# Inverse roots of the first attention's norms: from GpSimd's power to ScalarE's logarithm and exponential with a Newton step on VectorE

## Chip, core and metric

One core of a Trainium2 chip runs the whole program. The metric is the device time of one execution in microseconds, as a median over runs.

## What is computed

Attention with normalised queries and keys, followed by a feed-forward block with a squared ReLU:

```python
def rmsnorm(x, g):
    rms = np.sqrt(np.mean(x * x, axis=-1, keepdims=True) + 1e-06)
    return x / rms * g
q_n, k_n = (rmsnorm(q, g_q), rmsnorm(k, g_k))        # (8, 12, 448, 64)
scores = 1.0 / np.sqrt(64) * np.matmul(q_n, k_n.transpose(0, 1, 3, 2))
attn = softmax(scores)                                # over the keys
x = np.matmul(attn, v)                                # -> (8*448, 12*64)
out = np.maximum(x @ w_in, 0.0) ** 2 @ w_out          # 768 -> 2048 -> 768
```

The change concerns 1 / rms, the inverse root of the mean square over 64 values of a head's row, for queries and keys.

## The kernel before

Heads are handled in pairs: 8 batches x 6 pairs make 48 pairs. Two batches form a span; there are four spans. The first span's attention (pairs 0 to 11, `attention_alone`) runs by itself at the start of the program; the attention of each later span is interleaved with the second matrix product of the span before it, where TensorE is full of other work. The order of all instructions is written out by hand (`manual_schedule`): each engine takes its own instructions in program order, and semaphores hold an instruction until what it reads or overwrites is ready.

Both matrix products of the feed-forward block use a two-level scheme with seven products instead of eight, and the weight blocks for it (sums and differences of quarters) are made on the chip during the first attention and the first product. The generator `prepare(t)` hands this work out in four ticks a step: ScalarE takes absolute values and scales (L578, L594), VectorE works on exponents and signs (L591, L596, L601), GpSimd joins the words (L566) and adds blocks (L572), and SP writes finished blocks to DRAM (L586). The loop around `attention_alone` calls `weights(...)` at every `yield`, so these ticks are strewn through the iterations.

An iteration i of `attention_alone`, on TensorE: scores of key chunks 0 and 1 (L767), transposes of the normed keys of pair i+1 (L742), the values of pair i-1 for its last two chunks (L825), transposes of the normed queries of pair i+1 (L742), scores of chunks 2 and 3, the softmax totals of pair i-1 (L850, six matmuls for odd i and four for even i, each recorded twice by the profile), the values of pair i for its first two chunks. Scores live in two banks, so the scores of the next iteration wait for the exponentials of chunks 2 and 3. ScalarE takes in the same iteration, in this order: exponentials of chunks 0 and 1 (L771, four instructions), the copy of the transposed keys out of PSUM (L744), the squares for pair i+2 (L698), the copy of the transposed queries (L746), exponentials of chunks 2 and 3; the weights' ticks fall between. The transposed keys and queries of a pair share one PSUM bank, so the transposes of the queries wait for L744.

The norm of pair i+2 is made in iteration i by `norm`: ScalarE squares queries and keys (L698), VectorE sums over 64 (L699) and scales and adds epsilon (L700), GpSimd takes the power -0.5 of the 16 columns (L702) and multiplies the queries by it (L704); the keys' root is applied later as the scale of the exponentials. Pairs 0 to 2 use `normalise_in_turn` instead, with queries and keys one after the other; pairs from 12 on use `norm_by_squares`, which also has a power on GpSimd (L724) in another layout. Neither of the two is changed.

On VectorE an iteration also has the sums of probabilities (`add_up`, L784), and `finish` for pair i-1 (L863 to L874: transpose the totals, reciprocal, transpose back, multiply). `combine_x` (L884, L887 to L889) prepares sums of inputs for the first product from pair 6 on.

At the start of the program a 1x1 exponential (L1229) makes ScalarE load its table before data is there.

Of the kernel before, what the change touches and what calls it, by code (L numbers as in the profile page):

```python
# [2 lines left out]

# [6 lines left out]
F32 = mybir.dt.float32  # L10
U32 = mybir.dt.uint32
AF = mybir.ActivationFunctionType
ALU = mybir.AluOpType
# [290 lines left out]
def places_of(qk, i, work):  # L304


    first, second = i % 2 * 4 + work, i % 2 * 4 + 2 + (i // 2 + work) % 2
    return qk[:, first:second + 1:second - first]
# [78 lines left out]
def attention_then_ffn_bounded(  # L387
# [35 lines left out]
    nc = tc.nc  # L423

    B, H, S, D = q.shape
    NT, DM = out.shape
    DFF = w_in.shape[1]
    P = 128
    NJ = 4
    SP = S // NJ  # L430
# [11 lines left out]
    NAT = 2 * NPAIR  # L442
# [9 lines left out]
    small = ctx.enter_context(tc.tile_pool(name="small", bufs=2))  # L452
# [11 lines left out]
    qk, qkT, ident, mhalf, gains, rstd0, _ = held  # L464
# [189 lines left out]
    vs, probs, pavs, tots, normed, rstds = {}, {}, {}, {}, {}, {0: rstd0}  # L654
    places, halves, rests = [], [], {}
    sums = {"out": [dram.tile([2 * S // 32, 32], F32, name=f"factors{n}") for n in range(2)]}
# [20 lines left out]
    def load_v(i):  # L677
        b, h0 = i // NPAIR, 2 * (i % NPAIR)
        vs[i] = loads.tile([P, 2, NJ, D], F32, tag="vt", name="vt")
        if i < NAT:  # L680
            nc.sync.dma_start(vs[i][:SP].rearrange("p h j d -> p h (j d)"),
                              v[b, h0:h0 + 2].rearrange("h (p j) d -> p h (j d)", j=NJ))
        else:
            for h in range(2):
                nc.sync.dma_start(vs[i][:, h, 0:NF], v[b, h0 + h, 0:NF * P].rearrange("(j p) d -> p j d", j=NF))
            for rows in sides:
                nc.sync.dma_start(vs[i][rows, :, NF], v[b, h0:h0 + 2, NF * P:].rearrange("h p d -> p h d"))

    def norm(i):
        if i >= NAT:  # L690
            squares(i)
            return norm_by_squares(i)
        raw, sq = (places_of(qk, i, n)[:SP] for n in range(2))
        rstd = rstds[i] = small.tile([SP, 2, 2 * NJ], F32, tag="rstd", name="rstd", bufs=4)
        normed[i] = sq[:, 0], raw[:, 1]
        if i <= 2:
            return normalise_in_turn(nc, raw, sq, rstd, mhalf)
        nc.scalar.activation(sq, raw, AF.Square)  # L698
        nc.vector.tensor_reduce(rstd, sq.rearrange("p s (n d) -> p s n d", d=D), AX, ALU.add)  # L699
        nc.vector.tensor_scalar(rstd, rstd, 1.0 / D, 1e-6, ALU.mult, ALU.add)  # L700
        flat = rstd.rearrange("p s n -> p (s n)")
        nc.gpsimd.tensor_tensor(flat, flat, mhalf[:SP, 0:4 * NJ], ALU.pow)  # L702

        nc.gpsimd.tensor_tensor(sq[:, 0].rearrange("p (j h d) -> p h j d", j=NJ, h=2),  # L704
                                raw[:, 0].rearrange("p (h j d) -> p h j d", j=NJ, h=2),
                                rstd[:, 0].rearrange("p (h j) -> p h j ()", h=2).to_broadcast([SP, 2, NJ, D]),
                                ALU.mult)
# [131 lines left out]
    def added(i):  # L839

        return 3 if i % 2 and i + 1 < NAT else 2
# [49 lines left out]
    def attention_alone():  # L891


        for i in range(NAT):
            more = i + 1 < NAT
            if 0 < i < NAT - 3:
                load(i + 3)
            scores(i, 0)
            scores(i, 1)
            if i == 0:  # L900

                transpose(1, 1, 1)
                scores(0, 2)
                scores(0, 3)
                transpose(1, 0, 0)
                add_up(0, 1)
                norm(2)
                load_v(1)
                values(0, (0, 1))
                load(3)  # L910
                yield
                continue
            if more:
                transpose(i + 1, 1, 0)
            values(i - 1, (2, 3))
            add_up(i, 1)
            if i + 2 < NAT:
                norm(i + 2)
            elif not more:
                norm(NAT)  # L920
                load(NAT + 2)
            yield
            if more:
                transpose(i + 1, 0, 0)
            load_v(i + 1)
            yield
            scores(i, 2)
            scores(i, 3)
            total_of(i - 1)
            values(i, (0, 1))  # L930
            finish(i - 1)
            yield
            if added(i) == 3:
                add_up(i, 2)
            combine_x(i - 1)
            if NAT <= i + 3 < NAT + 2:
                load(i + 3)
            yield
        values(i, (2, 3))
        total_of(i)  # L940
        finish(i)
        combine_x(i)
# [185 lines left out]
    with tc.tile_pool(name="words", bufs=2) as spare["pool"]:  # L1128
        load(2)
        for _ in range(2):  # L1130
            load_w(loaded[0])
            loaded[0] += 1
        norm(1)
        with tc.tile_pool(name="first", bufs=2, reuse_waits="tile") as work:

            free = [gT[:, f] for f in range(NFC) if f % HF < HF - 2]
            places[:] = [g.rearrange("p (h q) -> p h q", h=2) for g in free[:2 * NJ]]
            sums[0], sums[1] = (g.rearrange("p (h q) -> p h q", h=2) for g in free[2 * NJ:2 * NJ + 2])
            sums["turned"], sums["factors"] = (g[:, 0:S] for g in free[2 * NJ + 2:2 * NJ + 4])
            sums["ones"] = work.tile([SP, D], F32, tag="ones", name="ones", bufs=1)  # L1140
            nc.vector.memset(sums["ones"], 1.0)
            for u, _ in enumerate(attention_alone()):

                weights(min(EARLY, 4 + (EARLY - 4) * u // (4 * NAT - 7)))
                if u == 4 * NAT - 9:
                    load_blocks(5)
        with tc.tile_pool(name="first_product", bufs=2, reuse_waits="tile") as work:
            for u, _ in enumerate(first_product(work, 0)):
                if u == 6:

                    left = ps_s.tile([P, 2, 512], F32, tag="s", name="bits")
                    banks["bits"] = left.rearrange("p a b -> p (a b)")[:, 0:NW].bitcast(U32)
                weights(min(ALL, EARLY + (ALL - EARLY) * (u - 1) // (N1 - 6)))
                if u == N1 - 5:
                    norm(NAT + 1)
                if u == N1 - 4:
                    transposes(NAT)
                    squares(NAT + 2)
# [25 lines left out]
def kernel(  # L1184
# [17 lines left out]
    nc = tc.nc  # L1202
    S, D = q.shape[-2:]
    bound = ctx.enter_context(tc.tile_pool(name="bound", bufs=1))
    gg = bound.tile([1, 2, D], F32, name="gg")
    top = bound.tile([1, 1], F32, name="top")
# [18 lines left out]
    )  # L1225
    with tc.manual_schedule():

        nc.vector.memset(top, 0.0)
        nc.scalar.activation(top, top, AF.Exp)  # L1229
        first_pair(tc, q, k, g_q, g_k, held)  # L1230

    bits = nc.values_load(top.bitcast(mybir.dt.int32))
# [37 lines left out]
```

## Time and profile before

| what | us |
|---|---|
| median of 3 runs (lowest, highest) | 1368.19 (1366.46, 1371.15) |
| the profiled execution: its time | 1369.76 |
| the profiled execution: its span, first to last instruction | 1367.8 |
| TensorE busy in 20.00 to 66.28 us | 44.75 of 46.28 |
| TensorE busy in 66.28 to 109.50 us | 38.93 of 43.22 |
| TensorE busy in 109.50 to 137.00 us | 25.00 of 27.50 |
| TensorE busy in 137 to 262 us (first product) | 124.47 of 125.00 |
| TensorE busy from 262 us to the end | 1092.27 of 1105.80 |

The first attention lasts from about 9 us to 133 us. A row of the profile gives an engine's busy time; an idle engine is listed with what ended its wait, as read from the semaphores. Instructions that ran on TensorE have modelled ends, so a gap of a tenth of a microsecond is at the limit of what can be read.

The granted TensorE clock is full in every slice of the span. ScalarE's busy time in the first 133 us is made of these groups, among others (busy us, mean ns of one, then the idle time before them):

```profile
L771 ACT ACTIVATE gT<-sc,rstd 112x448 f32<-112x448 f32 x96 | 53.1, 645 | 14.7 <-PE sc L767 11.5 <-issue 1.7 <-POOL rstd L702 1.5
L698 ACT ACTIVATE qk<-qk 112x1024 f32<-112x1024 f32 x9 | 9.8, 1084 | 2.8 <-DMA qk<-in_k_dram 2.8
L746 ACT ACTIVATE qkT<-pt,gains 128x448 f32<-128x448 f32 x11 | 7.1, 646 | 3.3 <-PE pt L742 3.3
L744 ACT COPY qkT<-pt 128x448 f32<-128x448 f32 x11 | 6.0, 548 | 0.0
```

### The profile page before, as it was taken

How to read it: one execution, taken by the hardware profiler on the slowest of the kernel's cores; microseconds unless marked ns; L12 is line 12 of the kernel's file. 1: busy time of each engine (PE TensorE's matmuls, PEld its weight loads, DVE VectorE, ACT ScalarE, POOL GpSimd, SP SyncE). 2: the span in 40 equal slices, each digit the busy share in tenths (PEclk: the TensorE clock that was granted, in tenths of full speed). 3: DMA queues.
4: the chain of work that ended last, by engine and by line, in shares of the span. 5: the costliest groups of instructions: out<-in, count | busy, mean ns of one | idle time of the engine just before them, and what ended most of it. 6: DMA issues, size and time to landing. Idle time of an engine off the chain costs nothing.

```text
span 1367.8 us, 16894 instructions
## 1 busy us (share of the span) xinstructions
PE 1341.9 (98%) x5602; PEld 638.1 (47%) x5602; DVE 811.9 (59%) x1434; ACT 426.8 (31%) x657; POOL 633.2 (46%) x505
## 2 busy tenths in 40 slices
PE   8989999999999999999999999999999999999997
PEld 3333454444444455444444455444444445554553
DVE  6989776499986334467778523467788533332111
ACT  7875565433332011233332011233433101110000
POOL 6998887455563122555564122545666312220000
PEclk9999999999999999999999999999999999999999
DMA  9787998655675333446676433345765433333443
GB/s 245 194 234 198 329 390 291 184 117 118 133 141 126 97 86 87 102 113 136 130 140 121 111 93 87 100 110 106 157 124 114 99 91 89 90 90 101 106 114 66
DMA packets 434021, 190.12 MB, mean 139 GB/s; under 512 B 282885, under 2 KB 430725, under 8 KB 433925
## 3 DMA queue, kind: packets, MB, share of 16 engines
q1 hardware_dynamic: 425476, 180.10, 52.2%
q0 software_dynamic: 4736, 8.40, 2.4%
q8 instruction: 47, 0.77, 0.2%
q10 hardware_dynamic: 3712, 0.46, 0.2%
q14 instruction: 50, 0.40, 0.1%
HBM read 155.72 MB, written 33.16 MB: 138 GB/s over the span
## 4 chain that ended last, share of the span: by engine, by line
PE 86%; POOL 6%; DVE 4%; DMA 2%; issue 2%; ACT 1%; DVEq 0%; POOLq 0%; ACTq 0%
PE ps L1086 35%; PE pa L1039 10%; PE pd L1039 10%; PE pc L1039 10%; PE sc L759 7%; PE pav L836 6%; PE pb L1039 5%; POOL rstd L702 2%; POOL gC L566 1%; POOL gC L572 1%; DMA xT<-factors 1%; POOL qk L704 1%; DMA sw<-w1s 1%; ACT gT L771 0%; PE tot L850 0%
## 5 line engine op out<-in xcount | busy, mean ns | idle before, releaser
L1086 PE MATMUL ps<-gT,sw 128*128 128x448 f32 x768 | 301.1, 545 | 4.7 <-DVE p L1105 4.0
L1016 POOL TENSOR_TENSOR gT<-gT 128x448 f32<-128x448 f32 x96 | 93.9, 980 | 290.6 <-ACT gT L1012 290.6
L1086 PE MATMUL ps<-gC,sw 128*128 128x448 f32 x576 | 225.2, 542 | 0.0
L1086 PEld LDWEIGHTS ps<-gT,sw 128*128 128x128 f32 x768 | 144.4, 191 | 156.3 <-issue 145.6
L724 POOL TENSOR_TENSOR half<-half,mhalf 128x28 f32<-128x28 f32 x36 | 174.5, 4847 | 75.3 <-DVE half L723 72.1
L1086 PEld LDWEIGHTS ps<-gC,sw 128*128 128x128 f32 x576 | 108.0, 190 | 113.0 <-issue 110.1
L1039 PE MATMUL pa<-xT,sw 128*128 128x448 f32 x384 | 154.9, 539 | 0.0
L1012 ACT ACTIVATE gT<-gT 128x448 f32<-128x448 f32 x96 | 55.4, 577 | 311.6 <-DVE gT L1054 311.5
L761 ACT ACTIVATE pr<-sc 128x896 f32<-128x896 f32 x87 | 77.4, 915 | 121.5 <-PE sc L759 121.5
L759 PE MATMUL sc<-qkT 64*64 64x448 f32 (+1 forms) x1152 | 109.7, 496 | 0.0
L1039 PEld LDWEIGHTS pa<-xT,sw 128*128 128x128 f32 x384 | 72.9, 190 | 71.7 <-issue 70.3
L804 POOL DMA_DIRECT2D xT<-factors x72 | 38.0, 532 | 90.1 <-DMA factors<-square 61.0
L1054 DVE TENSOR_TENSOR gT<-z,pd 128x448 f32<-128x448 f32 x32 | 19.8, 620 | 99.7 <-PE pd L1039 99.6
L1039 PE MATMUL pb<-xC,sw 128*128 128x448 f32 x192 | 77.6, 540 | 1.4 <-issue 1.4
L1039 PE MATMUL pc<-xT,sw 128*128 128x448 f32 x192 | 77.5, 540 | 0.5 <-DMA sw<-w1s 0.5
L1039 PE MATMUL pd<-xT,sw 128*128 128x448 f32 x192 | 77.8, 541 | 0.0
L1039 PE MATMUL pc<-xC,sw 128*128 128x448 f32 x192 | 77.5, 540 | 0.0
L1039 PE MATMUL pd<-xC,sw 128*128 128x448 f32 x192 | 77.4, 539 | 0.0
L726 POOL TENSOR_TENSOR qk<-qk,half 128x448 f32<-128x448 f32 x72 | 75.0, 1061 | 2.8
L572 POOL TENSOR_TENSOR gC<-gC 128x384 f32<-128x384 f32 x64 | 73.2, 1162 | 2.5
L836 PE MATMUL pav<-pr,vt 64*64 64x448 f32 x348 | 72.7, 537 | 1.5 <-DVE half L872 1.5
L836 PE MATMUL rest<-pr,vt 64*64 64x448 f32 x348 | 72.7, 537 | 0.0
(135 smaller groups left out, 1879.7 us busy)
## 6 DMA issues: line engine op xcount, KB each, us to landing
sw<-w1s SPq DMA_DIRECT2D x224, 192.0 KB, 2.4
sw<-w2s SPq DMA_DIRECT2D x168, 256.0 KB, 3.2
w1s<-gC SPq DMA_DIRECT2D x8, 1344.0 KB, 7.5
w2s<-gC SPq DMA_DIRECT2D x8, 1344.0 KB, 8.1
out_dram<-osb SPq DMA_DIRECT2D x184, 56.0 KB, 1.9
qk<-in_q_dram SPq DMA_DIRECT2D x144, 56.0 KB, 3.6
qk<-in_k_dram SPq DMA_DIRECT2D x144, 56.0 KB, 2.9
xT<-factors POOLq DMA_DIRECT2D x72, 112.0 KB, 3.4
```

Source lines behind the costliest of these rows:

```text
L572: nc.gpsimd.tensor_tensor(*[blocks_of(n)[:, i] for i in (dst, x, y)], op)
L702: nc.gpsimd.tensor_tensor(flat, flat, mhalf[:SP, 0:4 * NJ], ALU.pow)
L724: nc.gpsimd.tensor_tensor(half, half, mhalf, ALU.pow)
L726: nc.gpsimd.tensor_tensor(qkn[:, s], raw[:, s], half[:, s * NG:(s + 1) * NG].rearrange("p g -> p g ()").to_broadcast([P, NG, 32]), ALU.mult)
L759: nc.tensor.matmul(sc[part, h, 0:n], qkT[rows, 0, 1, keys], qkT[rows, 0, 0, of], start=True, stop=True)
L761: nc.scalar.activation(pr, sc[:, :, 0:n], AF.Exp)
L804: nc.gpsimd.dma_start(xT[h * D:(h + 1) * D, b % 2, hp], sums["out"][i % 2].rearrange("(h g) t -> h () (g t)", h=2)[h].to_broadcast([D, S]))
L836: nc.tensor.matmul(into, vs[i][rows, h, c, :], probs[i, c][rows, h, :], start=(c == 0), stop=(c == NF), skip_group_check=True)
L1012: nc.scalar.activation(g, src, AF.Relu)
L1016: nc.gpsimd.tensor_tensor(g, g, g, ALU.mult)
L1039: nc.tensor.matmul(ps, stream[n + i][:, c], rhs[:, c], start=first and c == 0, stop=c == HC - 1, skip_group_check=not first)
L1086: nc.tensor.matmul(ps, stream[n][:, c % 4], rhs_of[i][:, c], start=c == 0, stop=c == HF - 1)
```

## The change

For pairs 3 to 11 `norm` ends after the scaling (L700). The roots and the product with the queries move to a new function `roots`, which is called one `yield` later in the same iteration, behind the transposes of the queries of pair i+1 and the load of v. There ScalarE computes ln(x / 2^63) and from it exp(-0.5 ln(x / 2^63) - 31.5 ln 2), which is the inverse root; VectorE improves it by one Newton step in three operations, y (1.5 - 0.5 x y^2); and GpSimd's product with the queries follows as before. Two small tiles are used for it, of the tags that `norm_by_squares` uses too. The bias of the exponential gets a tile of its own, set once by VectorE. At the start of the program the 1x1 memset and exponential are replaced by an explicit preload of the table set that has logarithm and exponential. Between `norm` and `roots` of the same pair lies one call of `weights`, so in most iterations a tick's instructions come between them on each engine.

```diff
@@ norm, pairs from 3 on
         nc.scalar.activation(sq, raw, AF.Square)
         nc.vector.tensor_reduce(rstd, sq.rearrange("p s (n d) -> p s n d", d=D), AX, ALU.add)
         nc.vector.tensor_scalar(rstd, rstd, 1.0 / D, 1e-6, ALU.mult, ALU.add)
+
+    def roots(i):
+        raw, sq = (places_of(qk, i, n)[:SP] for n in range(2))
+        rstd = rstds[i]
         flat = rstd.rearrange("p s n -> p (s n)")
-        nc.gpsimd.tensor_tensor(flat, flat, mhalf[:SP, 0:4 * NJ], ALU.pow)
-
+        y, t = (small.tile([P, 2 * S // 32], F32, tag=tag, name=tag)[:SP, 0:4 * NJ] for tag in ("half", "other"))
+        nc.scalar.activation(y, flat, AF.Ln, scale=2.0 ** -63)
+        nc.scalar.activation(y, y, AF.Exp, scale=-0.5, bias=sums["rebias"])
+        nc.vector.scalar_tensor_tensor(t, y, -0.5, flat, ALU.mult, ALU.mult)
+        nc.vector.tensor_tensor(t, t, y, ALU.mult)
+        nc.vector.scalar_tensor_tensor(flat, t, 1.5, y, ALU.add, ALU.mult)
         nc.gpsimd.tensor_tensor(sq[:, 0].rearrange("p (j h d) -> p h j d", j=NJ, h=2),
...
@@ attention_alone
             if more:
                 transpose(i + 1, 0, 0)
             load_v(i + 1)
+            if i + 2 < NAT:
+                roots(i + 2)
             yield
@@ before the loop over attention_alone
+            sums["rebias"] = work.tile([SP, 1], F32, tag="rebias", name="rebias", bufs=1)
+            nc.vector.memset(sums["rebias"], -31.5 * math.log(2.0))
@@ start of the program
-        nc.vector.memset(top, 0.0)
-        nc.scalar.activation(top, top, AF.Exp)
+        nc.scalar.preload_act_table_set("natural_log_exp_and_others")
```

More of the change, by code (lines that the diff above doesn't have):

```diff
@@ L1 @@
+import math
 import struct
```

## The prediction

> **What bounds the kernel now.** I read the page first (shares by engine, then the chain), then the waits of TensorE in the stage that the change touches, then that stage cut into its iterations, and last the timeline of the iterations that are too long. TensorE is busy for 98% of the span, so the most that any edit can give is its idle time, 1367.8 - 1341.9 = 25.9 us, and only the part of it that lies in the first attention. Columns below: busy us, share, instructions.
>
> ```profile
> PE 1341.9 (98%) x5602; PEld 638.1 (47%) x5602; DVE 811.9 (59%) x1434; ACT 426.8 (31%) x657; POOL 633.2 (46%) x505
> ```
>
> The next view has one row per iteration of the loop over pairs, here i = 2, 3, 4, 6, 7 and 8, each starting where TensorE starts the scores of the pair's chunk 0 (L767). (The third row is cut at 56.50; TensorE in fact starts i = 5 at 55.97.)
>
> ```profile
> core 0: us, PE busy (x) PEld busy (x) DVE busy (x) ACT busy (x) POOL busy (x), PEclk, DMA share, GB/s
> 27.43:36.69 9.26, 9.26 (x51) 3.59 (x49) 9.12 (x11) 7.83 (x13) 6.81 (x5) 1.00 1.15 266
> 36.69:46.71 10.02, 10.02 (x55) 3.90 (x53) 9.78 (x13) 8.62 (x14) 9.68 (x7) 1.00 0.53 161
> 46.71:56.50 9.79, 9.79 (x54) 3.93 (x54) 9.65 (x11) 7.85 (x13) 9.60 (x7) 1.00 0.37 119
> ...
> 66.28:76.09 9.81, 9.33 (x50) 3.59 (x48) 8.88 (x12) 8.22 (x14) 9.73 (x8) 1.00 0.36 119
> 76.09:87.73 11.64, 10.20 (x54) 3.88 (x53) 8.26 (x12) 8.56 (x14) 11.41 (x9) 1.00 1.09 288
> 87.73:99.30 11.57, 9.33 (x51) 3.60 (x49) 10.84 (x14) 7.95 (x13) 11.33 (x9) 1.00 1.09 297
> ```
>
> The reader should see two lengths at which TensorE has no gap: 9.26 us (even i, where the softmax total L850 has 8 records) and 10.02 us (odd i, 12 records). From i = 5 on the iterations are longer, and there GpSimd is busy without a break (11.41 of 11.64). Against these floors the starts 55.97, 66.28, 76.09, 87.73, 99.30, 109.50, 119.06 leave 0.29 + 0.55 + 1.62 + 2.31 + 0.18 + 0.30 = 5.25 us. What TensorE waited for between 18 and 140 us (sum, times, longest):
>
> ```profile
> PE pt L742 <- POOL qk L704: 4.6, 5, 2.2
> PE pt L742 <- ACT qkT L744: 2.0, 1, 2.0
> PE pb L1039 <- issue: 1.4, 1, 1.4
> PE tot L850 <- DVE gT L863: 0.8, 1, 0.8
> ```
>
> And how the worst of the five looks in the timeline: the power cannot start before the weights' work ahead of it on GpSimd is done, the product with the roots follows it, and TensorE's transpose follows that.
>
> ```profile
> 87.17 1.99 POOL L566 TENSOR_TENSOR gC<-words,gC 128x384 int32<-128x384 int32 x2
> ...
> 89.12 3.63 POOL L702 TENSOR_TENSOR rstd<-rstd,mhalf 112x16 f32<-112x16 f32 x1
> ...
> 92.82 1.04 POOL L704 TENSOR_TENSOR qk<-qk,rstd 112x512 f32<-112x512 f32 x1
> ...
> 93.92 0.60 PE L742 MATMUL pt<-ident,qk 112*128 112x112 f32 x4 [2.24 <-POOL qk L704]
> ```
>
> So in this stage GpSimd's queue is the bound from i = 5 on, TensorE before that. But VectorE is at 9.1 to 9.8 us of these same iterations, and ScalarE at 8 to 8.7: what is taken off GpSimd lands on engines with little room.
>
> **What the Trainium skill says.** "ScalarE: Activation LUTs", section "What ACT_TABLE_LOAD costs", prices an activation at 186 ns + 0.833 ns per element, 93 ns more for a pointer operand; section "Table sets: the hidden batching unit" says that one set holds exp and ln both. The trace of before agrees on the price (L1012, 448 elements: 186 + 373 = 559, measured 577) and shows one table load of 1283 ns at the start; that the logarithm runs without a second load no trace shows yet, but the changed program has one load too. "SBUF — State Buffer", section "Who interferes with whom": a VectorE instruction with two SBUF inputs, or a copy or tensor_scalar in its fast mode, shares a port with GpSimd and waits for the other to finish; tensor_reduce does not. The trace agrees, first by the line of the sums of probabilities, then by the tile of the roots (min/median/max ns):
>
> ```profile
> L784 DVE TENSOR_TENSOR gT<-gT x17: 1026/1487/1935, 13.8 to 125.6; 112x896 f32<-112x896 f32 x17
> ```
>
> ```profile
> L699 DVE TENSOR_REDUCE rstd<-qk x9: 1204/1208/1220, 22.9 to 104.2; 112x16 f32<-112x1024 f32 x9
> L700 DVE TENSOR_SCALAR rstd<-rstd x9: 174/375/807, 24.2 to 105.4; 112x16 f32<-112x16 f32 x9
> L702 POOL TENSOR_TENSOR rstd<-rstd,mhalf x9: 2896/3142/3750, 24.4 to 109.1; 112x16 f32<-112x16 f32 x9
> L704 POOL TENSOR_TENSOR qk<-qk,rstd x9: 1041/1044/1739, 27.6 to 112.1; 112x512 f32<-112x512 f32 x9
> ```
>
> The sums of L784 swing between 1.03 and 1.94 us, the reduction does not move.
>
> **The change, part by part.**
>
> Removed: nine powers on GpSimd, 28.4 us of its time between 24.4 and 112. GpSimd is then no longer full (some 9.7 - 3.15 = 6.5 us an iteration), its product L704 comes right after the roots, and its weights' work and the write of the finished blocks, behind which SP holds the next loads of q and k, come earlier. I take the whole 5.25 us as gone. Not below 4.6 us, the listed waits, unless something else is late; not above 5.25.
>
> The tail. Nothing of GpSimd is removed after pair 11, but its backlog is. VectorE works without a gap from 117.67 to 137, and TensorE waits for it twice there (0.83 for L863, and 1.44 before pb, which needs the bank that L874 of the last pair reads until 136.68). In this stretch L591, L887, L888, L889 took 1.03, 1.42, 1.33, 1.44 us, beside L572 and L566 on GpSimd; uncontended they are 0.55 and three times 0.63 (132.35 to 134.2). That is 2.9 us. With the power gone GpSimd's L704 of pair 11 comes about 5 us earlier, so these sums should run alone. The gain is between 0 and 2.27 us (the two waits); I take 1.5.
>
> Added on ScalarE: a logarithm and an exponential for each of nine pairs, right behind L746 in its queue. Prices: 0.20 and, with the bias pointer, 0.29 us (page above, 16 elements; the 1x1 exponential in this trace took 202 ns). They depend on each other, so some 0.55 us, 5 us in all. But the logarithm also waits for VectorE: after the square L698 ends, reduction and scaling take 0.08 + 1.22 + 0.03 + 0.17 = 1.50 us at best, while L746 ends about 0.5 us after L698 (32.14 and 32.66). Behind the waiting logarithm stand the weights' L594 or L578 and the exponentials of chunks 2 and 3, and for those the score banks and TensorE's next scores. Worked from E, the start of the exponentials of chunk 0: L744 at +2.1, L698 from +2.5 to +3.6, scaling done at +5.1, logarithm and exponential until +5.65, one weights' operation to +6.5, exponentials of chunks 2 and 3 to +8.6, the second weights' operation to +9.45. The next E, if TensorE has no gap, is 9.26 or 10.02 later. So ScalarE is 0.19 us late in an even iteration and 0.57 early in an odd one. The transpose of q waits for L744, which ends 0.1 us ahead of TensorE (40.46 and 40.57), so every tenth that ScalarE is late is TensorE's. A weights' operation between L698 and L746 changes nothing in the sum.
>
> That holds if VectorE comes at once. In before the scaling ended on average 2.2 us after L698 (1.5 to 3.4), because L784 and L700 were held by GpSimd. Call the lateness x. Then TensorE loses 0.19 + x in an even iteration and x - 0.57 (not below 0) in an odd one. On average x was thus 0.7 in before. GpSimd keeps its heavy work, some 6.5 us of each iteration, but gets pauses, so I take x = 0.6: 0.8 and 0, over four iterations of each kind 3.2 us; I put it at 3.5. Bounds: x = 0 gives 0.8 us, x = 1.8 gives 4 x (2.0 + 1.2) = 12.9 us.
>
> Added on VectorE: three dependent operations on 16 columns, 0.19 us each by L722 and L723 (0.188 and 0.178 on 28 columns), 0.66 us with their gaps, 6 us in all. In most iterations one weights' operation stands between the scaling and them and covers the 0.6 us of ScalarE; for pair 8 there is none. VectorE had 0.2 us of room an iteration at i = 2 to 4 and about 1 us later, contention included. Two of its inputs are in SBUF, so each can also be held by GpSimd. I count that within x; it is the same lateness.
>
> Nothing: the first memset and 1x1 exponential go, and a preload takes the place of the table load that stood there (1.28 us, over at 2.01, data for the square at 3.34). The memset of the bias is one small operation on VectorE. TensorE's and SP's queues keep their order.
>
> Sum: -5.25 - 1.5 + 3.5 = -3.25 us. The profiled run took 1369.76 us, 1.96 outside its span; minus 3.25 that is 1366.5. It lies 1.6 above the median of the three runs, 1368.19, against which the result will stand: 1365.0.
>
> **The rivals.** About 0.3%, 4.1 us, is what a measurement here can tell from nothing.
>
> Forecast, a part of GpSimd's waits kept as gain: 1365.0, from 1362 to 1367.5. Chance 0.42.
>
> Everything hidden: x near 0 and the tail takes its 2.27: -5.25 - 2.27 + 0.5 = -7, 1361. For it speaks that the room on ScalarE was real (11.5 us waiting for TensorE, eight times); against it, VectorE's 97% at i = 2 to 4. Chance 0.20.
>
> The wait only changes its owner: VectorE keeps its 9.65 us of i = 2 to 4 and gets 0.66 and a wait of 0.2 on top, 10.5 against a floor of 9.64 on average; eight iterations cost 7, the gain is 6.75: 1368.4. The same time would come if the first product, with DMA at 0.90 and one wait of 0.53 us for sw, ate what attention saved. Chance 0.20.
>
> Slower: ScalarE's in-order queue. If the scaling comes x later than its best, every logarithm holds the exponentials of chunks 2 and 3, and with them TensorE. The loss outgrows the gain of 6.75 from x = 1.03 and reaches +0.3% at x = 1.54; at x = 1.8 it is +6.2, 1374.4. For it: two of nine scalings in before had x above 1 (1.15 and 1.9), one 0.96. Against: GpSimd has a third less to do. In it I count 0.02 for the case that the change does not do what it says, and tables are loaded at each switch (18 x 1.28 = 23 us, 1391). Chance 0.18.
>
> **How the numbers follow.** Faster by over 0.3% means below 1364.1: all of the second case and a third of the first, 0.35. Slower, above 1372.3: most of the last and a little of the third, 0.19. The rest 0.46. The range leaves out the tail of the last case and of the second: 1360.5 to 1373. The forecast's own range is 1362 to 1367.5.
>
> **What would show it.** Right: no wait of L742 for GpSimd's product; one table load; iterations i = 6 to 8 at 9.3 to 10.3 us; ScalarE's logarithm idle for 1 to 2 us before it, for VectorE's scaling; even iterations i = 2 and 4 somewhat longer than 9.26. The tail step is right if L887 to L889 take 0.63 us and the waits before L850 and pb shrink. Wrong: i = 2 to 4 at 10.5 us or more with VectorE full, or new waits of TensorE for L744 at every i; or L1039's waits for sw growing.

## The result, and the profile after

The changed kernel took 1365.83 us in the median of 22 runs (1361.83 to 1368.88), the kernel before 1368.9 us in the runs beside it. The ratio is 0.9975, with a 95% interval of 0.9968 to 0.9982: 3 us less, a little less than the bound of 0.3%. The forecast was 1365.0 us, a change within that bound. The time came out, but not by the sum that was written down, as the traces show. The profiled run took 1366.76 us, its span 1364.9.

First the busy times on the page of the changed kernel (us, share of the span, instructions):

```profile
PE 1341.6 (98%) x5602; PEld 637.3 (47%) x5602; DVE 813.1 (60%) x1461; ACT 430.0 (32%) x674; POOL 604.1 (44%) x496
```

GpSimd lost 29.1 us (633.2 before), ScalarE gained 3.2, VectorE 1.2; TensorE's work is the same. Next what TensorE waited for between 18 and 140 us in the changed kernel (sum, times, longest). Lines have moved: L753 is the transpose that was L742, L755 the copy that was L744, L778 the scores (L767), L782 the exponentials (L771), L795 the sums of probabilities (L784), L1052 the first product (L1039).

```profile
PE pt L753 <- ACT qkT L755: 3.8, 6, 1.9
PE sc L778 <- ACT gT L782: 2.2, 3, 1.0
PE pb L1052 <- PE pa L1052: 0.7, 1, 0.7
```

The 4.6 us for GpSimd's product are gone, every one of them. In their place stand waits for ScalarE's copy of the keys (L755) and for its exponentials: 1.9 us of the first line are the wait of pair 1 that was there before (2.0), the other 1.9 and the 2.2 for exponentials are new. The wait before pb, one of the partial sums of the first product, fell from 1.4 to 0.7; that of the totals for VectorE (0.8) is gone. The same stage by iterations, here i = 2, 4, 6, 7 and 8, each from the first scores of its pair:

```profile
core 0: us, PE busy (x) PEld busy (x) DVE busy (x) ACT busy (x) POOL busy (x), PEclk, DMA share, GB/s
29.16:38.42 9.26, 9.26 (x51) 3.59 (x49) 8.29 (x13) 7.14 (x14) 1.65 (x2) 1.00 0.85 230
48.43:58.56 10.13, 9.33 (x50) 3.60 (x49) 9.89 (x15) 7.63 (x15) 8.07 (x6) 1.00 0.77 209
69.12:78.94 9.82, 9.37 (x50) 3.59 (x48) 9.06 (x13) 7.73 (x15) 7.74 (x6) 1.00 0.94 293
78.94:90.34 11.40, 10.31 (x53) 3.81 (x53) 10.93 (x18) 9.42 (x17) 6.20 (x7) 1.00 0.81 254
90.34:100.84 10.50, 9.37 (x51) 3.57 (x49) 10.17 (x14) 7.88 (x16) 6.60 (x5) 1.00 0.49 142
```

GpSimd is at 8 us or less and no longer the bound. Yet the iterations together are as long as before. From the first scores of pair 2 to those of pair 11 it took 91.83 us (29.16 to 120.99), in the kernel before 91.63 (27.43 to 119.06). The floor of these nine iterations, without a gap on TensorE, is 5 x 9.26 + 4 x 10.02 = 86.38. I call this stretch the loop. Before, 5.25 us of it were lost to GpSimd; now 5.45 are lost to something else. The timeline of i = 4 shows to what:

```profile
51.98 1.10 ACT L699 ACTIVATE qk<-qk 112x1024 f32<-112x1024 f32 x1
...
52.80 1.90 DVE L795 TENSOR_TENSOR gT<-gT 112x896 f32<-112x896 f32 x1
...
53.71 1.87 POOL L567 TENSOR_TENSOR gC<-words,gC 128x384 int32<-128x384 int32 x1
...
54.62 1.21 DVE L700 TENSOR_REDUCE rstd<-qk 112x16 f32<-112x1024 f32 x1
...
55.86 0.17 DVE L701 TENSOR_SCALAR rstd<-rstd 112x16 f32<-112x16 f32 x1
...
56.07 0.22 ACT L710 ACTIVATE half<-rstd 112x16 f32<-112x16 f32 x1 [2.47 <-DVE rstd L701]
56.32 0.31 ACT L711 ACTIVATE half<-half,rebias 112x16 f32<-112x16 f32 x1
...
57.36 2.20 ACT L782 ACTIVATE gT<-sc,rstd 112x448 f32<-112x448 f32 x4
...
58.56 2.06 PE L778 MATMUL sc<-qkT 64*112 64x448 f32 x8 [0.80 <-ACT gT L782]
```

The square ends at 53.08. VectorE is then in the middle of a sum of probabilities, 1.90 us long where it takes 1.08 at its shortest, and starts the reduction only at 54.62. The scaling ends at 56.03, 1.45 us later than the best case of 1.50 after the square: that is the x of the prediction. ScalarE stood 2.47 us at the logarithm, the exponentials of chunks 2 and 3 stood behind it, and TensorE's next scores came 0.80 us late. Over the first 133 us the groups by line show the price of each new operation (us in total, mean ns, then idle time before it and its cause):

```profile
L711 ACT ACTIVATE half<-half,rebias 112x16 f32<-112x16 f32 x9 | 2.8, 308 | 0.3
L710 ACT ACTIVATE half<-rstd 112x16 f32<-112x16 f32 x9 | 1.9, 216 | 15.6 <-DVE rstd L701 15.6
L713 DVE TENSOR_TENSOR other<-other,half 112x16 f32<-112x16 f32 x9 | 1.6, 175 | 0.3
L714 DVE SCALAR_TENSOR_TENSOR rstd<-other,half 112x16 f32<-112x16 f32 x9 | 1.6, 175 | 0.3
L712 DVE SCALAR_TENSOR_TENSOR other<-half,rstd 112x16 f32<-112x16 f32 x9 | 1.6, 174 | 1.6 <-ACT half L711 1.6
```

The operations are as cheap as foreseen; the wait of the logarithm, 15.6 us in nine times, is three times as long as both of ScalarE's operations together (4.7 us). What did gain is the stretch behind the loop, from the first scores of pair 11 to the first product's pb, 17.72 us before and 15.91 after. The timeline of VectorE there, with TensorE's pb as last line:

```profile
122.07 0.70 DVE L592 TENSOR_SCALAR gC<-gC 128x768 f32<-128x768 f32 x1
...
122.69 1.44 DVE L898 TENSOR_TENSOR xC<-xT,xC 128x448 f32<-128x448 f32 x1
...
124.15 0.62 DVE L899 TENSOR_TENSOR xC<-xT,xC 128x448 f32<-128x448 f32 x1
124.70 0.62 DVE L900 TENSOR_TENSOR xT<-xT 128x448 f32<-128x448 f32 x1
...
136.90 2.49 PE L1052 MATMUL pb<-xC,sw 128*128 128x448 f32 x6 [0.69 <-PE pa L1052]
```

These four operations took 5.22 us before and take 3.38 now. Before, GpSimd worked until 124.73 us and all three adds ran beside it from 121.08 on; now it stops at 123.64 and only the first add, at 122.69, meets it. That is 1.84 us, the size by which this stretch, the tail, became shorter (1.81).

The two spans should not be compared as wholes. In these two profiles pb starts at 136.78 us before and at 136.90 after, so the attention as a whole ends no earlier: the 1.61 us that loop and tail gained went to a slow window of TensorE's clock in pair 1 (last section), which the first profile of the kernel before does not have. The 2.8 us between the two spans lie behind pb, in stages that the change does not touch. Over all thirteen profiles the time from pb to the end lies between 1225.7 and 1231.0 us.

### The profile page after: what moved, and what is told of

It reads as the page before. It is cut to its first block, busy times and chain, and to the rows that moved or that the text cites. A ratio compares the mean times of both kernels' runs of the same rounds, so it can differ in the third digit from the quotient of the medians.

```text
span 1364.9 us, 16882 instructions
## 1 busy us (share of the span) xinstructions
PE 1341.6 (98%) x5602; PEld 637.3 (47%) x5602; DVE 813.1 (60%) x1461; ACT 430.0 (32%) x674; POOL 604.1 (44%) x496
## 4 chain that ended last, share of the span: by engine, by line
PE 86%; DVE 5%; ACT 3%; issue 2%; DMA 2%; POOL 2%; SPq 0%; POOLq 0%; DVEq 0%; ACTq 0%
PE ps L1099 36%; PE pd L1052 10%; PE pc L1052 10%; PE pa L1052 10%; PE sc L770 7%; PE pav L847 7%; PE pb L1052 5%; DMA sw<-w1s 1%; ACT gT L782 1%; DVE gT L795 1%; POOL gC L573 1%; POOL gC L567 1%; DVE rstd L700 1%; PE sc L778 0%; PE tot L861 0%
## 5 line engine op out<-in xcount | busy, mean ns | idle before, releaser
L1052 PE MATMUL pa<-xT,sw 128*128 128x448 f32 x384 | 154.9, 539 | 0.8 <-DMA sw<-w1s 0.8
L1052 PEld LDWEIGHTS pa<-xT,sw 128*128 128x128 f32 x384 | 72.8, 190 | 72.8 <-issue 72.3
L1052 PE MATMUL pd<-xC,sw 128*128 128x448 f32 x192 | 77.5, 539 | 0.8 <-DVE gC L602 0.8
L1052 PE MATMUL pb<-xC,sw 128*128 128x448 f32 x192 | 77.5, 539 | 0.7 <-PE pa L1052 0.7
L1052 PE MATMUL pc<-xC,sw 128*128 128x448 f32 x192 | 77.5, 540 | 0.6 <-DMA sw<-w1s 0.6
L1052 PE MATMUL pd<-xT,sw 128*128 128x448 f32 x192 | 77.8, 541 | 0.0
L573 POOL TENSOR_TENSOR gC<-gC 128x384 f32<-128x384 f32 x64 | 76.4, 1212 | 2.5
L1052 PE MATMUL pc<-xT,sw 128*128 128x448 f32 x192 | 77.4, 539 | 0.0
```

Source lines behind the costliest of these rows:

```text
L573: nc.gpsimd.tensor_tensor(*[blocks_of(n)[:, i] for i in (dst, x, y)], op)
L1052: nc.tensor.matmul(ps, stream[n + i][:, c], rhs[:, c], start=first and c == 0, stop=c == HC - 1, skip_group_check=not first)
```

## The experiments

**Theory A**: taking the power off GpSimd gives the whole 5.25 us, and the logarithm's wait for VectorE, in ScalarE's in-order queue, takes it back. **Rival B**: the loop is bound by something that neither touches, such as the weights' work or the loads, and the relief of GpSimd is worth little. **Rival C**: VectorE is full, and its three new operations cost the time themselves. In the table, all stretches are us in the profiled run; loop and tail are the two stretches above; "lost" is the loop less 86.38; the wait of the logarithm is that between 27 and 120 us; x is the prediction's lateness, the end of the scaling beyond its best case of 1.50 us after the square, as a mean over pairs 3 to 11. A field is empty where the value was not worked out.

| kernel | median (range, runs) | ratio to before, 95% | loop | lost | tail | logarithm's wait | x |
|---|---|---|---|---|---|---|---|
| before | 1368.19 (1366.46 to 1371.15, 3) | | 91.63 | 5.25 | 17.72 | none | 0.70 |
| after | 1365.83 (1361.83 to 1368.88, 22) | 0.9975, 0.9968 to 0.9982 | 91.83 | 5.45 | 15.91 | 13.9 | 1.00 |
| after_again | 1366.73 (1363.94 to 1369.23, 20) | 0.998, 0.9971 to 0.999 | 91.80 | 5.42 | 15.94 | 14.0 | |
| before_again | 1369.47 (1366.5 to 1372.73, 12) | 1.0002, 0.9991 to 1.0014 | 93.06 | 6.68 | 17.74 | none | 0.41 |
| no_power | 1361.88 (1359.23 to 1369.21, 17) | 0.9948, 0.9937 to 0.996 | 86.35 | 0 | 17.03 | none | 0.90 |
| both_ways | 1382.88 (1379.53 to 1383.22, 4) | 1.0089, 1.0064 to 1.0113 | 107.5 | 21.1 | 18.1 | 25.2 | |
| both_ways_2 | 1371.07 (1369.02 to 1374.32, 16) | 1.0019, 1.001 to 1.0028 | 98.9 | 12.5 | 16.98 | 13.0 | 1.26 |
| late_roots | 1372.88 (1368.0 to 1378.92, 20) | 1.003, 1.0018 to 1.0042 | 98.14 | 11.8 | 16.8 | 1.9 | 2.20 |
| mid_roots | 1364.95 (1362.86 to 1371.86, 20) | 0.9979, 0.997 to 0.9989 | 90.54 | 4.2 | 16.51 | 8.9 | 1.61 |
| no_newton | 1361.45 (1360.18 to 1363.54, 4) | 0.995, 0.9934 to 0.9967 | 89.63 | 3.3 | 15.53 | 9.8 | 0.52 |
| log_ready | 1363.3 (1361.02 to 1367.27, 11) | 0.9962, 0.9946 to 0.9977 | 86.65 | 0.3 | 19.46 | none | 1.92 |
| lean | 1362.22 (1361.18 to 1364.82, 6) | 0.9953, 0.9936 to 0.9969 | 88.77 | 2.4 | 15.54 | 7.6 | |
| lean_mid | 1359.0 (1358.28 to 1360.96, 4) | 0.9921, 0.99 to 0.9943 | 86.42 | 0 | 15.54 | 2.8 | |

**The changed kernel, profiled once more (after_again).** No edit; how far does a single profile bind?

> The changed kernel once more, for a second profile. The two first profiles show a loop over pairs that is not shorter (scores of pair 2 to scores of pair 11: 91.63 us before, 91.83 after), in which GpSimd's waits (4.6 us) have gone and ScalarE's have come (3.8 + 2.2 us, 2.0 of them in both); the tail from there to the first product's pb went from 17.72 to 15.91. Theory A (waits changed their owner in the loop; the gain is the tail's): loop 91 to 92 us again, tail 15.5 to 16.5. Rival B (the first profile was a poor draw, the loop did gain 2 to 4 us): loop 88 to 89.5. Time 1365 to 1366.5 in both.

The loop took 91.80 us and the tail 15.94, against 91.83 and 15.91. So in this kernel the two stretches repeat from one profile to the next, while whole spans of single profiles differ by 2 us through other stages.

**The power taken out and nothing put in its place (no_power).** Against the kernel before; the products take the mean square where the inverse root belongs, so the root is what this kernel leaves out.

```diff
-        nc.gpsimd.tensor_tensor(flat, flat, mhalf[:SP, 0:4 * NJ], ALU.pow)
```

> The kernel before, with GpSimd's power of pairs 3 to 11 left out and nothing in its place: queries and keys of these pairs are multiplied by the mean square instead of its inverse root. It measures the relief of GpSimd alone. By the prediction's sum (5.25 of the loop and 1.5 of the tail): ratio to before 0.995, some 1361.5 us; loop 86.4 to 87.5 us, no wait of the transposes for GpSimd, no wait for ScalarE either except in pair 1. Rival (VectorE is a bound of its own beside GpSimd): the loop stays above 89 us and the ratio above 0.997.

Its iterations i = 5, 7 and 8, columns as above:

```profile
57.70:67.72 10.02, 10.02 (x55) 3.89 (x53) 8.46 (x12) 7.84 (x13) 6.55 (x6) 1.00 0.73 203
...
76.97:86.99 10.02, 10.02 (x55) 3.89 (x53) 9.85 (x11) 8.30 (x14) 9.86 (x8) 1.00 0.97 269
86.99:96.25 9.26, 9.26 (x51) 3.60 (x49) 9.12 (x11) 7.83 (x13) 6.58 (x6) 1.00 1.08 288
```

Every iteration is at its floor. The loop went from 91.63 to 86.35: 5.28 us, where the prediction had 5.25. Rival B falls. The iteration i = 7 is at its floor with GpSimd busy for 9.86 of 10.02 us: here a full engine is no bound by itself, as long as nothing that TensorE waits for comes late. And x is 0.90 without any of the new operations, so VectorE is late by its old work; before, nothing stood in ScalarE's queue to be held by that.

**Both ways at once (both_ways, both_ways_2).** GpSimd keeps its power and its product for the queries and ScalarE and VectorE do the new sequence beside it, its result unused. The scaling writes a tile of its own that both read. The edit, cut to its main lines, is against the changed kernel.

```diff
-        nc.vector.tensor_scalar(rstd, rstd, 1.0 / D, 1e-6, ALU.mult, ALU.add)
+        means[i] = small.tile([SP, 2, 2 * NJ], F32, tag="means", name="means", bufs=1)
+        nc.vector.tensor_scalar(means[i], rstd, 1.0 / D, 1e-6, ALU.mult, ALU.add)
+        nc.gpsimd.tensor_tensor(rstd.rearrange("p s n -> p (s n)"), means[i].rearrange("p s n -> p (s n)"),
+                                mhalf[:SP, 0:4 * NJ], ALU.pow)
...
-        flat = rstd.rearrange("p s n -> p (s n)")
+        flat = means[i].rearrange("p s n -> p (s n)")
```

> GpSimd keeps its power and gives the roots as before; the logarithm, the exponential and the three VectorE operations of the changed kernel are made as well, in the same places, and their result is not used. It measures the added work alone. By the prediction's sum (x = 0.6 or more, now with GpSimd full): 3.5 to 6 us slower than before, ratio 1.0025 to 1.0045, with waits of the transposes for both GpSimd and ScalarE. Rival (ScalarE and VectorE have room, the additions are hidden): ratio 0.9995 to 1.001.

This run can't be used for the question. The last of the new operations wrote its result over the power's input, and so had to wait for the power. The waits of VectorE in it between 27 and 120 us (sum, times, longest):

```profile
DVE means L719 <- POOL rstd L703: 18.7, 8, 2.7
```

These 18.7 us are a wait that neither kernel has. In both_ways_2 that operation writes its scratch tile instead:

```diff
-        nc.vector.scalar_tensor_tensor(flat, t, 1.5, y, ALU.add, ALU.mult)
+        nc.vector.scalar_tensor_tensor(t, t, 1.5, y, ALU.add, ALU.mult)
```

> The added work alone again: as both_ways, but the last VectorE operation writes to a tile of its own and not over the power's input, so that VectorE no longer waits for GpSimd's power (18.7 us in eight times there). By the changed kernel's loss against no_power (5.5 us in the loop), with GpSimd full on top: 3 to 8 us slower than before, ratio 1.002 to 1.006. If the wait for the power was all that both_ways cost: ratio 0.9995 to 1.001.

The ratio is 1.0019: the new sequence on top of the old one costs 0.19%, 2.6 us, against the kernel before. The loop of its profile is at 98.9 us; two windows at half clock (6.8 us long together) cost up to 3.4 of these, which leaves about 95.5, 3.9 above the kernel before. It lost about 9.1 us, less than the two sequences by themselves (5.25 + 5.45 = 10.7) but much more than either: the two overlap only in part.

**The roots placed later (late_roots).** The call goes behind the finish of the pair before, so that the logarithm finds its input ready.

```diff
             load_v(i + 1)
-            if i + 2 < NAT:
-                roots(i + 2)
...
+            if i + 2 < NAT:
+                roots(i + 2)
```

> The changed kernel with the roots of a pair called later in the same iteration, after the exponentials of chunks 2 and 3 on ScalarE and after the division of the outputs on VectorE, so that the logarithm finds its input ready. If ScalarE's stand at the logarithm (15.6 us in nine times) is what gives the loop's gain back: no such stand, waits of TensorE for ScalarE down from 6.0 to about 2 us, loop 87.5 to 89 us, ratio to before 0.994 to 0.9955. If VectorE's load is the bound: loop 90.5 us or more, ratio as for the changed kernel, 0.997 to 0.998. If the roots now come too late: a wait of the transposes for GpSimd's product of over 2 us in all.

The wait of the logarithm fell from 13.9 to 1.9 us, and the kernel became slower: 1372.88 us. TensorE's waits between 18 and 140 us:

```profile
PE pt L753 <- POOL qk L715: 8.4, 5, 3.8
PE pt L753 <- ACT qkT L755: 3.0, 1, 3.0
```

The three operations of the Newton step now stand on VectorE behind the finish, GpSimd's product behind them, and TensorE's transpose waits for that. There is a latest place as well as an earliest. (Two windows at half clock, 6.8 us long together, cost up to 3.4 of the 11.8 us that its loop lost.)

**The kernel before, profiled once more (before_again).** No edit.

> The kernel before, for a second profile. In the profile before, scores of pair 2 to scores of pair 11 took 91.63 us, from there to pb 17.72, from pb to the first scores of the next span 125.48, and TensorE lost 4.0 us to waits for VectorE's sum p later on. The changed kernel repeats its own loop to 0.03 us (91.83 and 91.80). If the changed kernel's gain is the tail alone: loop 91.4 to 91.9, tail 17.5 to 18, time within 0.1% of before, and the later waits for p near 1.4 us as in the changed kernel. If more of the gain is in the loop: loop 93 us or more.

The loop took 93.06 us, 1.4 more than in the first profile, and one iteration holds it. Its iterations i = 7 and 8:

```profile
78.04:89.72 11.68, 10.23 (x55) 3.88 (x53) 8.29 (x12) 8.61 (x14) 11.44 (x9) 1.00 1.09 287
89.72:102.92 13.20, 10.97 (x51) 3.91 (x49) 10.84 (x14) 8.04 (x13) 12.96 (x9) 0.87 1.09 297
```

The granted clock of the second is 0.87. The first profile had 11.57 us there at 1.00, with the same wait for GpSimd. TensorE's timeline where it begins:

```profile
95.89 0.60 PE L742 MATMUL pt<-ident,qk 112*128 112x112 f32 x4 [2.23 <-POOL qk L704]
96.42 2.70 PE L767 MATMUL sc<-qkT 64*112 64x448 f32 x8
```

The eight scores took 2.70 us, where they take 1.76 at full clock. Without this window the loop is 93.06 - 1.63 = 91.4 us: the 91.63 of the first profile stand. The clock of all runs is counted below.

**The three operations of VectorE taken out (no_newton).** The exponential writes the roots; the Newton step is left out.

```diff
-        nc.scalar.activation(y, y, AF.Exp, scale=-0.5, bias=sums["rebias"])
-        nc.vector.scalar_tensor_tensor(t, y, -0.5, flat, ALU.mult, ALU.mult)
-        nc.vector.tensor_tensor(t, t, y, ALU.mult)
-        nc.vector.scalar_tensor_tensor(flat, t, 1.5, y, ALU.add, ALU.mult)
+        nc.scalar.activation(flat, y, AF.Exp, scale=-0.5, bias=sums["rebias"])
```

> The changed kernel without the three VectorE operations: the exponential's result is the root, without the Newton step. If the logarithm's wait for VectorE's scaling costs the loop, and not VectorE's three operations: scaling still late, loop 90.5 to 92 us, ratio to before 0.997 to 0.998. If VectorE's added work makes the scaling late: lateness x from 1.0 to 0.5 us or less, loop 88 to 90 us, ratio 0.9955 to 0.9965.

Three operations of 0.17 us and their gaps, some 0.6 us an iteration, made VectorE earlier by 0.48 us in the mean (x from 1.00 to 0.52), the logarithm's wait shorter by 4.1 us, the loop by 2.2. Rival C is thus a part of it, 2.2 of 5.45 us, and 3.25 us are lost without these operations.

**The roots between chunks 2 and 3 (mid_roots).** A place between the changed kernel's and that of late_roots.

```diff
             load_v(i + 1)
+            yield
+            scores(i, 2)
             if i + 2 < NAT:
                 roots(i + 2)
-            yield
-            scores(i, 2)
             scores(i, 3)
```

> The changed kernel with the roots called between the scores of chunks 2 and 3 of the same iteration: on ScalarE the logarithm stands behind the exponentials of chunk 2, some 1.1 to 2 us later than in the changed kernel, on VectorE the Newton step still stands ahead of the division of the outputs. If the stand at the logarithm costs the loop: idle time before the logarithm from 15.6 us to under 5, loop 87.5 to 89.5 us, ratio to before 0.994 to 0.9955. If a later place makes GpSimd's product late, as in late_roots: waits of the transposes for it of over 2 us, ratio 0.998 or more.

The loop took 90.54 us, outside what A expected (87.5 to 89.5). The logarithm waited 8.9 us in five times and not 13.9 in eight, but the longest wait stayed at 2.6, and it now holds the exponentials of chunk 3 alone, with less time left until TensorE needs them. The place by itself does not make up for VectorE's lateness. The time, 0.9979 of the kernel before, is that of the changed kernel (0.9975).

**The wait taken away and all work kept (log_ready).** The logarithm reads a tile of ones that is there from the start. It computes the same number of elements at the same place, but the roots are then not those of the means; that dependence is what it leaves out.

```diff
-        nc.scalar.activation(y, flat, AF.Ln, scale=2.0 ** -63)
+        nc.scalar.activation(y, sums["ones"][:, 0:4 * NJ], AF.Ln, scale=2.0 ** -63)
```

> The changed kernel, but the logarithm reads a column block of ones that is ready since the start, not the pair's mean squares; all instructions stay, in number and place (the roots are then the Newton step from 1, for mean squares near 1 close to the true ones). It takes away the logarithm's wait for VectorE's scaling and leaves the work on ScalarE and VectorE. If the stand at the logarithm is what costs the loop: no idle before it, loop 86.5 to 88 us, ratio to before 0.9935 to 0.995. If VectorE's added work costs it by itself: loop 89.5 us or more, ratio 0.996 or more.

For the loop, this is the run that decides. The loop took 86.65 us, 0.3 from its floor, with both operations of ScalarE and all three of VectorE in it, and with VectorE later than in the changed kernel: x is 1.92, not 1.00. So within the loop neither the work nor VectorE's lateness costs TensorE anything, as long as ScalarE's queue does not wait for it. There theory A stands, and what the wait costs the loop of the changed kernel is 91.83 - 86.65 = 5.2 us. But VectorE's work is not free: its lateness grows from 0.23 us at pair 3 to 4.41 at pair 11, and a part of it is paid behind the loop.

The ratio, 0.9962, missed what was expected (0.9935 to 0.995): the tail is 19.46 us, 3.5 longer than in the changed kernel. Its TensorE waits between 18 and 140 us, and the totals that stand behind the second line:

```profile
PE pt L753 <- ACT qkT L755: 2.4, 1, 2.4
PE tot L861 <- DVE gT L874: 2.2, 1, 2.2
PE pb L1052 <- PE pa L1052: 0.3, 1, 0.3
```

```profile
127.20 3.98 PE L861 MATMUL tot<-gT,ones 112*64 112x448 f32 x12 [2.20 <-DVE gT L874]
```

2.2 us are a wait for VectorE, which reaches pair 11 with more work behind it, and after it comes a window at half clock, in which the totals took 3.98 us; those of an earlier pair took 2.48. How much of this comes back in each run the one profile does not tell. Loop and tail together took 107.74 us in the changed kernel, 106.11 here (some 1.5 of it from the half clock), 105.16 in no_newton and 103.38 in no_power. So over both stretches the wait alone is worth 1.6 us, or 3.1 without the half clock, not 5.2; the median fell by 2.5. Of what remains above no_power the 2.2 us of waiting for VectorE are rival C's.

**Less in the chain (lean), and both steps together (lean_mid).** lean is no_newton with the scaling folded into the logarithm's own scale and bias, so that one operation of VectorE and one hand-over less stand ahead of ScalarE; lean_mid has the roots between chunks 2 and 3 as well. Both leave out the Newton step.

```diff
-        nc.vector.tensor_scalar(rstd, rstd, 1.0 / D, 1e-6, ALU.mult, ALU.add)
...
-        nc.scalar.activation(y, flat, AF.Ln, scale=2.0 ** -63)
+        nc.scalar.activation(y, flat, AF.Ln, scale=2.0 ** -63 / D, bias=sums["epsilon"])
```

> The changed kernel without the Newton step, and without VectorE's scaling (L701 there): the logarithm takes the sums with scale 2^-63/64 and bias 1e-6 x 2^-63. VectorE has then one operation less an iteration than the kernel before. no_newton has a loop of 89.63 us and ratio 0.995; the scaling's 0.2 us and its waits for the port are gone from the logarithm's wait: loop 87.5 to 89 us, ratio 0.9935 to 0.995, 1360 us. If the loop is no longer held by the logarithm: no change against no_newton.

> As lean, with the roots called between the scores of chunks 2 and 3, so that the exponentials of chunk 2 stand ahead of the logarithm. If the wait at the logarithm is what is left: idle before it near 0, loop 86.5 to 88 us, ratio 0.9925 to 0.9945. If the later product on GpSimd or the exponentials of chunk 3 take its place: loop as lean or longer.

lean's loop is 0.9 us shorter than no_newton's, its time not told apart from it (0.9953 and 0.995). lean_mid took 1359.0 us, 0.9921 of the kernel before (0.99 to 0.9943), the lowest median of all, over four runs. Its TensorE waits between 18 and 140 us, and the logarithm's:

```profile
PE pt L749 <- ACT qkT L751: 2.1, 1, 2.1
PE pb L1048 <- PE pa L1048: 0.3, 1, 0.3
```

```profile
ACT half L709 <- DVE rstd L700: 2.8, 4, 0.9
```

Only pair 1 and pb are left; the loop is at its floor. The logarithm's wait is 2.8 us, and no single one longer than 0.9: at that size it costs TensorE nothing. Against mid_roots the place is the same, with four operations of VectorE less; the reduction then starts 1.01 us late on average and not 1.54, and the place pays.

## Why the prediction was right, and where its sum was not

- **GpSimd's waits, -5.25.** Right: no wait for its product is left, and no_power measures the step by itself at 5.28.
- **The tail, -1.5.** Right in cause and nearly in size: 1.81 us, for which the four operations of VectorE, 1.84 us shorter, account. The Trainium skill's "SBUF — State Buffer", section "Who interferes with whom", fits here: an add of the same size takes 1.44 us beside GpSimd and 0.62 without. How much the relief brings depends on what GpSimd does just then: over the kernels without the power and with the logarithm's wait the tail was 15.5 to 16.8 us, in no_power 17.03, only 0.7 less than before.
- **Operations of ScalarE and VectorE.** Logarithm 0.216 and exponential 0.308 us against 0.20 and 0.29; Newton's three 0.175 against 0.19. The price of the Trainium skill's "ScalarE: Activation LUTs", section "What ACT_TABLE_LOAD costs", holds for 16 elements to within 9%. One table load of 1283 ns, so logarithm and exponential do share a set of tables, as its section "Table sets: the hidden batching unit" has it.
- **The mis-sized term, +3.5.** The mechanism was named (the logarithm holds the exponentials of chunks 2 and 3), and log_ready shows it; the size was not right. The step is "I take x = 0.6". Measured is 1.00 in the mean, from -0.04 to 1.86. The prediction's own formula gives 6.8 us for the measured values; the loop lost 5.45. I let x fall because GpSimd has a third less to do. But x isn't made by the power: no_power has 0.90, with a third less on GpSimd. It is made by the order on VectorE, where the reduction stands behind a sum that is held by whatever GpSimd does just then, and by the three new operations (0.48 of it, by no_newton). In the changed kernel such a sum stands right ahead of the reduction for all nine pairs; five of these sums took 1.76 to 1.90 us in place of 1.08.
- **A term that is missing, up to -1.5.** With -5.25, +5.45 and -1.8 the waits give -1.6 us, half of the 3 measured. For the other half there is a candidate, TensorE's clock, but no proof. Each run lists its span and mean granted clock; (1 - clock) x span, averaged, is 4.47 us over 52 runs of the kernel before, 2.98 over 22 of the changed one and 3.07 over the 20 of after_again. Not all of that is lost time: in every one of the thirteen profiles 1.0 to 2.3 us of it lie behind TensorE's last product, where it has nothing left to do. If that share is alike in both kernels, a difference of 1.4 to 1.5 us remains. The rest of the span went from 1362.47 to 1360.99 us, 1.48 less, which fits the 1.6 of the waits; in after_again it is 1361.52, 0.95 less. Another candidate are TensorE's waits for VectorE's tile p far behind pb, 4.0 and 2.4 us in the two profiles of the kernel before and 1.4 and 1.3 in those of the changed one; but other kernels with the same stages there have 0.2 (late_roots) to 3.0 (lean), so they vary with the execution. The sum had neither term. So the forecast hit 1365.0 by luck: its loop was 2 us too cheap, and something of nearly that size that it had not counted made up for it.
- **The signs to look for.** No wait for GpSimd's product, one table load, and a wait of 1 to 2 us at the logarithm (15.6 / 9 = 1.7): as written. Of the three adds of the tail two took 0.62 us, the first still 1.44. Iterations i = 6 to 8 at 9.3 to 10.3 us: right for the first, wrong for the others (11.40 and 10.50). Of i = 2 and 4 only the second became longer: the pair whose logarithm stands in i = 2 has x = -0.04. One of its signs of being wrong came in part: TensorE waited for the copy of the keys five times in the loop, 1.9 us in all.
- **The rivals.** Within the loop, "the wait only changes its owner" is what happened, mainly for another reason than given: log_ready has all of VectorE's work and its loop is at the floor. VectorE's work shows in no_newton's 2.2 us and in log_ready's tail.
- **Two slips.** The four operations of the tail were 5.22 - 2.44 = 2.78 us too long, not 2.9. And VectorE had 9.35 us an iteration at i = 2 to 4, with the third row ended at 55.97, not 9.65. Neither enters the 1365.0.

## What to carry to other kernels

A small operation moved to an engine with idle time costs what stands behind it in that engine's queue while it waits for its input; so look at when the input is ready, not at the room. Before moving work, remove its wait alone (give it ready data) and its work alone, and follow the gain past the stretch that you look at: here the wait was worth 5.2 us of the loop and VectorE's three operations 2.2, but with the wait gone the tail grew by 3.5. And when the input is late, first take work off the chain ahead of it, then choose the place: the place alone won 1.3 us of the loop, four operations of VectorE less 3.1, both together 5.4.

## What was not expected of the hardware

Waits of about 2 us on TensorE were sometimes followed by a window at half clock. The windows are 3.41 us long and cost up to 1.7 us each. In the changed kernel's first profile there is one in pair 1, columns as in the timelines above:

```profile
21.38 0.60 PE L753 MATMUL pt<-ident,qk 112*128 112x112 f32 x4 [1.94 <-ACT qkT L755]
21.91 2.95 PE L778 MATMUL sc<-qkT 64*112 64x448 f32 x8
```

The eight scores took 2.95 us in place of 1.76. The kernel before had the same wait (1.95) in its first profile without such a window. It has one much later, from 1099.41 to 1102.82 us, behind a wait of 1.96 us for VectorE's p; a digit of the page stands for 34 us and hides it, so the clock was not full in every slice, as was said ahead of the prediction.

The traces tell why a wait has this effect in some executions only. The windows lie on a fixed grid: each begins a whole number of times 3.413 us after the first record of the clock, in the second profile of the kernel before at 4.95 + 5 x 3.413 = 22.02 and at 4.95 + 27 x 3.413 = 97.11 us. What decides is how long TensorE was idle within the one window of the grid before it. These are the windows at pair 1's wait, first in the kernel before, then in the changed one:

```profile
core 0: us, PE busy (x) PEld busy (x) DVE busy (x) ACT busy (x) POOL busy (x), PEclk, DMA share, GB/s
17.38:20.79 3.41, 1.96 (x12) 0.58 (x10) 2.25 (x5) 3.41 (x7) 1.80 (x2) 1.00 1.18 269
20.79:24.21 3.42, 2.91 (x16) 1.36 (x18) 3.35 (x5) 3.42 (x7) 1.12 (x1) 1.00 1.09 347
```

```profile
18.93:22.34 3.41, 1.48 (x10) 0.67 (x8) 3.31 (x7) 3.41 (x7) 1.88 (x1) 1.00 1.11 324
22.34:25.75 3.41, 3.41 (x12) 1.09 (x10) 3.15 (x8) 1.70 (x5) 0.00 (x0) 0.50 1.09 349
```

In the kernel before, the edge at 20.79 cuts the wait in two, 1.45 and 0.51 us, and the clock stays full. In the changed one all 1.93 us fall into one window, and the next is at half clock. In the thirteen profiles, up to TensorE's last product, all 17 windows with 1.85 us of idle time or more were followed by one at half clock, and of the others with a full clock only one was, with 1.78 us (mid_roots; one with 1.80 was not). Two half-clock windows, after 3.41 and 3.28 us of idle time, had a second one behind them. The ends of TensorE's work are modelled, so the limit is good to a tenth at best. The grid starts 4.95 to 7.66 us into the span, differently in each execution, so the same wait costs 1.7 us more in one and nothing more in another.

The Trainium skill's "TensorE: Matmul & The Clock Gate", section "What's actually happening", describes a free-running window of 3413 ns and half the rate after an idle one. Length and grid agree; that about 1.8 us of idle time within a window is enough, not a whole idle window, is what these runs show.

Over all runs of a kernel, (1 - clock) x span was between 2.71 us (lean_mid) and 6.17 us (late_roots, which has waits of up to 3.8 us). Waits outside the loop count as well: no_power, with none in its loop, has 3.52, and its profile shows a window behind pair 1's wait of 1.9 us, one at 1093.95 behind a wait of 2.1 for p, and 1.25 us behind the last product.
